# Chunked linear attention and a mixture of experts on one core: domain probabilities over ScalarE's queue, loads in the order of chunks, and a new order of work

## The chip, the cores and the metric

The kernel runs on one core of a Trainium2 chip. TensorE (PE) multiplies matrices into PSUM; VectorE (DVE), ScalarE (ACT) and GpSimd (POOL) do the elementwise work; SyncE (SP) issues nearly all DMAs. Each engine works through its own list of instructions in order, and waits on semaphores for the others. The metric is the device time of one execution in microseconds (us). Three runs of the kernel before took 286.79, 284.99 and 287.0 us: median 286.79. One more execution was recorded by the profiler.

## The reference

Five inputs feed a linear attention with a state (4 batches, 8 heads, 768 positions, head size 48), whose output goes through a mixture of 4 experts (3072 rows of 384, inner size 1024):

```python
for t in range(S):
    kt, vt, rt = k[:, :, t], v[:, :, t], r[:, :, t]
    cur = einsum('bhd,bhe->bhde', u[None] * kt, vt)
    y[:, :, t] = einsum('bhd,bhde->bhe', rt, state + cur)
    state = w[None, :, :, None] * state + einsum('bhd,bhe->bhde', kt, vt)
x = y.transpose(0, 2, 1, 3).reshape(B * S, H * D)
p = domain_probs / (domain_probs.sum(-1, keepdims=True) + 1e-09)
for e in range(E):
    out += p[:, e:e + 1] * (maximum(x @ w1[e], 0.0) @ w2[e])
```

## The kernel before, in words

**Attention.** The sequence is cut into 24 chunks of 128 positions: chunk `ci` is batch `ci % 4`, place `ci // 4`. A chunk needs its r, k and v, 192 KB each (L271). r and k are multiplied by powers of w (`scale`, L433 or L438, on DVE; for chunks 1 to 3 partly on POOL) and turned (`T`): chunks 0 to 7 by PE transposes (L502) and a copy out of PSUM (`Tout`, L80 on ACT or L82 on DVE), later ones by a DMA transpose (L483). `At` is the product of k and r per head (L550), on half the height of the array. `mask` (L564, L567) keeps the upper triangle. `Y` multiplies it by v in bf16 (`Vb`, L80 on ACT or L84 on POOL) and adds the state's part (L590, L597). The u term goes over POOL and DVE: `ruk_a` (L450), `ruk_b` (L458), `dcoef` (L471), `dv` (L476); `Yout` (L612) adds dv to Y. `Sm` (L666), `Sv` and `S` carry the state on.

**Experts.** The first six chunks ("plain": chunks 0 to 3 together, 4 and 5 as halves) are transposed on PE (`X`, L649) and copied (`Xout`); `l1` is x @ w1 (L756, L762, L1180), `relu` its copy on ACT (L771, L773, L1185), `l2` the product with w2 (L792, L1197), and `ev` (L736, L738) multiplies by p and adds. The other chunks are multiplied by p first (`Xs`, L626, into four buffers in two halves that each chunk reuses) and turned by DMA (`Xout`, L637); they form stages 2 to 5 of four chunks and stage 6 of two. There the second product is made of products `P` with sums of weights (`mix`, L860) and sums of activations (`sum`, L933), L969 on PE, in the order of SEQ_2 to SEQ_5. w1 and w2 come in pieces (w1e0.1 is piece 1 of expert 0's w1; L288, L291) into four staging buffers, and are cast to bf16 by ACT, DVE or POOL (`cast`).

**p.** `prow`, 24 rows of 512 numbers (48 KB), is loaded by SP (L302) after the w2 pieces of expert 0. `pt` (L384) turns it by four fp32 transposes on PE, and `pn` (L388 to L391) normalises it on DVE.

**Order.** No order is written out by hand. Everything is a job with the engines that can do it, a rank, needs and buffers, and a planner in the kernel (L1249 to L1404) goes through an imagined time and hands each free engine the ready job of the lowest rank; what it makes is then issued as it stands. So ranks (`NUDGE` adds to some), the list of loads `ORDER`, and `GATES` (which job of the experts a pair of later chunks has to wait for) change the order on all engines. Where the planner sees PE without work in the first 20 us, it fills in spin matmuls (L247) that compute nothing (L1410 to L1418); they are instructions like others, and run whether or not the next job is ready.

```python
            if t < 20 and n > 0:
                spin(n, 1)
```

Of the kernel before, what the change touches and what calls it, by code (L numbers as in the profile page):

```python
# [19 lines left out]
def kernel(  # L20
# [121 lines left out]
    GATES = [0, 9, 1, 3, 15, 23, 26, 26]  # L142
# [16 lines left out]
    for n, sc in enumerate(ORDER_SC):  # L159
        CH0[sc], SC_AT[sc], X_AT[sc] = ci, at, n % 2  # L160
        for x in range(2 if sc == 6 else 4):
# [32 lines left out]
    SEQ_4 = ((0, 1, 0), (1, 1, 0), (0, 2, 0), (0, 2, 1), (0, 1, 1), (0, 7, 0), (0, 6, 0), (0, 6, 1), (0, 7, 1),  # L194
             (0, 5, 0), (0, 5, 1), (1, 2, 0), (1, 1, 1), (0, 3, 0), (0, 3, 1), (0, 4, 0), (0, 4, 1), (1, 2, 1),
             (1, 7, 0), (1, 6, 0), (1, 6, 1), (1, 7, 1), (1, 5, 0), (1, 5, 1), (1, 4, 0), (1, 4, 1), (1, 3, 0),
             (1, 3, 1))
    SEQ_5 = ((0, 1, 0), (1, 1, 0), (0, 7, 0), (0, 1, 1), (2, 2, 2), (1, 1, 1), (0, 6, 0), (0, 6, 1), (1, 7, 0),
             (2, 2, 1), (0, 7, 1), (2, 2, 7), (0, 5, 0), (0, 5, 1), (1, 6, 0), (2, 2, 4), (0, 4, 0), (1, 6, 1),
             (0, 4, 1), (1, 7, 1), (2, 2, 6), (0, 3, 0), (1, 5, 0), (1, 5, 1), (1, 4, 0), (2, 2, 5), (1, 3, 0),  # L200
             (1, 4, 1), (2, 2, 3), (0, 3, 1), (1, 3, 1))
# [11 lines left out]
             ('l1', 3, 1, 0, 1): -20, ('l1', 3, 6, 6, 2): 8, ('sum', 6, 1, 2, 1): -20, ('C', 6, 1, 2): 20}  # L213
# [39 lines left out]
    def load_job(name, nbytes_us, run, takes=(), needs=()):  # L253
        q_rank[0] += 1
        job(name, {"S": 0.5}, run, needs, q_rank[0], takes, (), nbytes_us)
# [3 lines left out]
    def load_in(n, ci):  # L259
# [12 lines left out]
        load_job((n, ci), (0.965, 64), run, (("inp", ci),))  # L272
# [28 lines left out]
    def load_p():  # L301
        load_job("prow", (0.36, 2), lambda: nc.sync.dma_start(  # L302
            prow, moe_domain_probs.rearrange("(n p) e -> n p e", p=C)))

    ORDER = ("K0 K1 R0 R2 R1 V0 K2 w1e0.1 w1e0.0 w1e0.2 V1 K3 V2 R3 w2e0.0 V3 w2e0.1 w2e0.2 p K4 w1e1.1 "
             "w1e1.0 R4 w2e1.0 w1e1.2 R5 V4 w2e1.1 w2e1.2 K5 K6 K7 K8 R9 R13 R6 w1e2.2 V5 K11 w1e3.2 "
             "w1e3.0 V12 V6 R7 w1e3.1 K10 R8 w2e2.1 K9 R16 w1e2.0 w1e2.1 K18 K15 V7 w2e2.0 w2e2.2 R12 V9 "
             "V16 R10 R17 R15 V14 V8 K14 K17 R18 w2e3.0 w2e3.1 w2e3.2 V17 V11 K13 R11 V10 V13 V15 K16 R14 "
             "K12 V18 " +
             " ".join(f"c{i}" for i in range(19, TOTC))).split()  # L310
    for what in ORDER:
        if what == "p":
            load_p()
        elif what[0] == "c":
            for n in ("Rt", "Kt", "Vt"):
                load_in(n, int(what[1:]))
        elif what[0] in "RKV":
            load_in(what[0] + "t", int(what[1:]))
        else:
            for i in ([int(what[5:])] if what[4:] else range(len(PIECES))):  # L320
                load_w(int(what[1]), int(what[3]), i)
# [58 lines left out]

    def c_pt():
# [11 lines left out]
    job("pt", {"T": 0.15}, c_pt, ["prow"], 0, (("mm", "pp"),))  # L393
    job("pn", {"V": 1.1}, c_pn, ["pt", ("Yout", SUB - 1)], 3.0, (), (("mm", "pp"),))
# [646 lines left out]
    def mix2(m, k):  # L1041
# [13 lines left out]
        needs = all_cast + [("Yout", ci) for ci in range(TOTC - SUB, TOTC)] +             ([("mix", 4, hf) for hf in range(2)] if m == 4 else [])  # L1055
# [10 lines left out]
    def level2(sc, at0):  # L1066
# [4 lines left out]
        def one(m):  # L1071
# [5 lines left out]
            def summed2(k, hf):  # L1077
# [10 lines left out]
                needs = all_cast + [("Yout", ci) for ci in range(TOTC - 2, TOTC)] + [("relu", e, sc, fb, 0) for e in (2 * hf, 2 * hf + 1) for fb in range(NFB)] +                     ([("sum2", sc, m, {3: 1, 2: 3, 4: 2}[k], hf)] if k != 1 else [])  # L1088
# [220 lines left out]
    def start(e):  # L1309
# [16 lines left out]
        if got is not None and now < HURRY:  # L1326

            us = got.on[e]
            for i in soon[e]:
                if i.name not in gone and i.rank < got.rank and fits(i) and                         now < known[i.name] < now + 0.6 * us:  # L1330
# [123 lines left out]
```

## Time and profile before

| what | us |
|---|---|
| median of three runs | 286.79 |
| lowest and highest of them | 284.99, 287.0 |
| the profiled execution's own time | 284.42 |
| its span, first to last instruction | 282.6 |
| PE busy (share of the span) | 277.0 (98%) |
| ACT, DVE, POOL busy | 188.4, 182.7, 112.2 |
| granted TensorE clock, mean | 0.999 |
| spin matmuls, all before 19 us | 95 |

Times in the profile are us from the start of the span. Busy time of PE takes in spins, and the ends of matmuls are modelled, so small gaps between them show only as the distance from one start to the next. A row of the waits names who waited, for whom, and total, times and longest. In the timeline and the chain of waits a row begins with start and duration.

### The profile page before, as it was taken

The numbers are of one execution on the slowest core, as the hardware profiler recorded it, in microseconds if no ns is written. First come the engines' busy times: TensorE is split into PE (matmuls) and PEld (weight loads), VectorE is DVE, ScalarE is ACT, GpSimd is POOL, SyncE is SP. The second block draws the span as 40 slices with busy tenths as digits, with TensorE's granted clock in tenths as the row PEclk, the third lists the DMA queues.
The fourth block names the chain that finished last, engine by engine and source line by source line (L and its number), as shares of the span: only waits on it lengthen the run. The fifth ranks groups of instructions, "written<-read, shape, count | busy, mean of one in ns | idle before, by whom it ended". The sixth has DMA issues, their size and how long they took to land.

```text
span 282.6 us, 6933 instructions
## 1 busy us (share of the span) xinstructions
PE 277.0 (98%) x2794; PEld 200.3 (71%) x2794; DVE 182.7 (65%) x313; ACT 188.4 (67%) x351; POOL 112.2 (40%) x129
## 2 busy tenths in 40 slices
PE   8989999999999999999999999999999999999995
PEld 3778567675865445899445899445899544999895
DVE  5976879875687667786347786167785353681061
ACT  4775946898652788655988656879653799612840
POOL 2884456882527565357463346264230000000000
PEclk9999999999999999999999999999999999999999
DMA  7999999999999999493993494965539110401001
GB/s 159 287 247 322 252 273 263 260 264 202 264 201 251 208 199 204 81 165 86 201 209 76 83 171 77 209 127 102 96 70 162 62 28 0 77 25 70 30 14 44
DMA packets 133491, 43.23 MB, mean 153 GB/s; under 512 B 121658, under 2 KB 133436, under 8 KB 133460
## 3 DMA queue, kind: packets, MB, share of 16 engines
q1 hardware_dynamic: 133300, 42.74, 70.0%
q8 instruction: 22, 0.36, 0.5%
q14 instruction: 9, 0.07, 0.1%
q10 hardware_dynamic: 160, 0.05, 0.1%
HBM read 26.79 MB, written 4.72 MB: 112 GB/s over the span
## 4 chain that ended last, share of the span: by engine, by line
PE 88%; DMA 5%; SPq 3%; DVE 1%; ACT 1%; issue 0%; POOL 0%; DVEq 0%; ACTq 0%
PE hT_ps L762 32%; PE M_ps L969 29%; PE out_ps L792 8%; DMA Vt<-in_v_dram 4%; PE hT_ps L1180 4%; PE hT_ps L1214 4%; PE out_ps L1197 3%; SPq L271 2%; PE Y_ps L597 2%; PE At_all L550 2%; PE hT_ps L756 1%; PE Y_ps L590 1%; PE St_ps L666 1%; DMA RKin<-in_r_dram 1%; PE M_two L1127 1%; PE RKT_ps L502 1%
## 5 line engine op out<-in xcount | busy, mean ns | idle before, releaser
L773 ACT ACTIVATE hAll<-hT_ps 128x512 bf16<-128x512 f32 x152 | 88.5, 598 | 13.6 <-PE hT_ps L762 8.6
L762 PE MATMUL hT_ps<-stg,w_sb 128*128 128x512 bf16 x384 | 86.7, 379 | 0.1
L762 PEld LDWEIGHTS <-w_sb 128*128 128x128 bf16 x456 | 42.8, 98 | 48.1 <-issue 0.4
L969 PEld LDWEIGHTS <-hAll 128*128 128x128 bf16 x832 | 68.5, 98 | 1.0
L626 ACT ACTIVATE stg<-dv,p_nat 128x384 bf16<-128x384 f32 x72 | 41.6, 609 | 12.6 <-DMA stg<-stg 6.8
L450 POOL TENSOR_TENSOR ruk<-RKin 128x384 f32<-128x384 f32 x24 | 27.1, 1129 | 41.9 <-DMA RKin<-in_k_dram 21.6
L969 PE MATMUL M_ps<-w_sb,hAll 128*128 128x192 bf16 x400 | 37.6, 246 | 0.0
L1004 ACT COPY o_sb<-M_ps 128x192 f32<-128x192 f32 x35 | 11.1, 317 | 37.4 <-PE M_ps L969 37.3
L476 POOL TENSOR_TENSOR dv<-Vt,dcoef 128x384 f32<-128x384 f32 x24 | 24.6, 1024 | 26.5 <-ACT stg L626 25.3
L458 POOL TENSOR_TENSOR ruk<-ruk,U_sd 128x384 f32<-128x384 f32 x23 | 26.5, 1153 | 1.4
L685 POOL TENSOR_TENSOR S<-Tn,wC 64x192 bf16<-64x192 f32 x32 | 21.4, 669 | 13.7 <-DVE Tn L675 12.2
L933 DVE TENSOR_TENSOR hAll<-hAll 128x1024 bf16<-128x1024 bf16 (+1 forms) x30 | 24.2, 825 | 0.2
L792 PE MATMUL out_ps<-w_sb,hAll 128*128 128x384 bf16 x128 | 23.9, 326 | 0.0
L933 DVE TENSOR_TENSOR stg<-hAll 128x1024 bf16<-128x1024 bf16 (+1 forms) x15 | 12.7, 847 | 15.3 <-ACT hAll L1222 11.5
L438 DVE TENSOR_TENSOR RK_sb<-RKin,W_both 128x768 bf16<-128x768 f32 x16 | 17.1, 1078 | 7.8 <-DMA RKin<-in_r_dram 4.7
L969 PE MATMUL M_ps<-o_sb,hAll 128*128 128x192 bf16 x216 | 21.6, 246 | 0.0
L969 PE MATMUL M_ps<-w_mix,hAll 128*128 128x192 bf16 x216 | 21.1, 246 | 0.0
L933 DVE TENSOR_TENSOR hAll<-stg,hAll 128x1024 bf16<-128x1024 bf16 (+1 forms) x15 | 12.6, 851 | 9.8 <-PE M_ps L969 9.6
L567 DVE TENSOR_TENSOR AtM<-At_all,mask 128x1024 bf16<-128x1024 f32 x8 | 9.8, 1221 | 12.6 <-PE At_all L550 12.6
L762 PE MATMUL hT_ps<-xTe,w_sb 128*128 128x512 bf16 x72 | 17.2, 379 | 0.0
L1006 DVE TENSOR_TENSOR o_sb<-o_sb,M_ps 128x192 f32<-128x192 f32 x25 | 8.8, 350 | 11.7 <-PE M_ps L969 9.4
L792 PEld LDWEIGHTS <-hAll 128*128 128x128 bf16 x128 | 11.6, 98 | 6.3
(110 smaller groups left out, 377.3 us busy)
## 6 DMA issues: line engine op xcount, KB each, us to landing
stg<-in_moe_w_dram SPq DMA_DIRECT2D x16, 576.0 KB, 6.2
RKin<-in_k_dram SPq DMA_DIRECT2D x24, 192.0 KB, 3.5
RKin<-in_r_dram SPq DMA_DIRECT2D x24, 192.0 KB, 3.6
Vt<-in_v_dram SPq DMA_DIRECT2D x24, 192.0 KB, 4.3
out_dram<-o_sb SPq DMA_DIRECT2D x23, 192.0 KB, 2.2
stg<-in_moe_w_dram SPq DMA_DIRECT2D x8, 384.0 KB, 5.7
stg<-stg SPq DMA_TRANSPOSE x36, 2.8
RKT<-RK_sb SPq DMA_TRANSPOSE x16, 3.5
```

The source lines that it names most:

```text
L438: job(("scale", ci, 0), {"V": SCALE_US}, lambda: nc.vector.tensor_mul(RK[:, :, :, 0:D], tl["in", ci], W_both), [("Rt", ci), ("Kt", ci), (" ...
L450: nc.gpsimd.tensor_mul(tl["ruk", ci], tl["Rt", ci], tl["Kt", ci])
L458: nc.gpsimd.tensor_mul(tl["ruk", ci], tl["ruk", ci], U_sd)
L476: nc.gpsimd.tensor_mul(tl["dv", ci], tl["Vt", ci], tl["dcoef", ci].to_broadcast((128, H, D)))
L626: nc.scalar.mul(o, tl["Ysb", ci], p_nat[:, e, n_p:n_p + 1])
L685: nc.gpsimd.tensor_mul(S_new[pr, :, cl], Tn2[pr, tn_at[ci], :, cl], wC[pr, :, None].to_broadcast((P2, NP, D)))
L762: nc.tensor.matmul(ps[:, 0:n, :].rearrange("p a b -> p (a b)"), w1_sb[:, e, db, fb * 128:(fb + 1) * 128], xTe[:, x0 + db, s0:s0 + n, :].re ...
L773: nc.scalar.activation(hTs[:, fb, s0:s0 + n, :], ps[:, 0:n, :], AF.Relu)
L792: nc.tensor.matmul(ps, relu_tile(e, sc)[:, fb, s, :], w2_sb[:, e, fb, :], start=(fb == 0), stop=(fb == NFB - 1))
L933: nc.vector.tensor_tensor(o, x, y, op=op)
L969: nc.tensor.matmul(tl["P", sc, q, m], st, moving(m, hf, (n + 4) % 8), start=(opens and n == 0), stop=(hf == 1 and n == 7), skip_group_chec ...
L1180: nc.tensor.matmul(ps[:, f, :], w1_sb[:, e, db, (a + f) * 128:(a + f + 1) * 128], get_xTe(1)[:, db, s, :], start=(f == 0 and db == 0), sto ...
```

## The change

p is no longer an entry of `ORDER` on SP: ACT issues its load right after the logarithm of w. `pt` waits for `umm` as well, its planned cost goes from 0.15 to 0.85, and it gets a pad of 2.2 us in the planner; `pn` no longer waits for `Yout` of chunk 3. Each load of r, k or v from chunk 5 on now comes behind the same load of the chunk before. `ORDER`, `GATES`, SEQ_2 to SEQ_5 are given anew (SEQ_5 keeps its second level), nine entries are added to `NUDGE`. The other edits only break long lines.

In the planner's order on the engines this does the following. In PE's, pt goes from between chunk 0's l2 pieces to between T(1,0) and Y(0), and the first l1 of expert 0 from between At(1) and At(2) to behind Y(1). On POOL dv(0) goes behind ruk_b(1), two scales, ruk_a(2) and ruk_b(2). On DVE pn goes ahead of chunk 1's masks. There are 93 spins for 95. SP's list is the same up to the last w2 piece of expert 0.

```diff
-    GATES = [0, 9, 1, 3, 15, 23, 26, 26]
+    GATES = [3, 9, 0, 11, 6, 5, 7, 30]
...
-    SEQ_4 = ((0, 1, 0), (1, 1, 0), (0, 2, 0), (0, 2, 1), (0, 1, 1), (0, 7, 0), (0, 6, 0), (0, 6, 1), (0, 7, 1),
...
+    SEQ_4 = ((0, 1, 0), (0, 2, 0), (0, 2, 1), (0, 1, 1), (0, 7, 0), (1, 1, 0), (0, 6, 0), (0, 6, 1), (0, 7, 1),
...
-             ('l1', 3, 1, 0, 1): -20, ('l1', 3, 6, 6, 2): 8, ('sum', 6, 1, 2, 1): -20, ('C', 6, 1, 2): 20}
+             ('l1', 3, 1, 0, 1): -20, ('l1', 3, 6, 6, 2): 8, ('sum', 6, 1, 2, 1): -20, ('C', 6, 1, 2): 20,
+             ('Wsb', 1): -2, 'lnr': 2.1, ('dv', 0): 27.8, ('Xout', 1): 14.5, ('mask', 2, 0): -4,
+             ('T', 3, 0): -11.8, ('Sm', 15): -20, ('mix', 2, 0): 20.1, ('l1', 0, 0, 6, 3): -9.1}
...
-    def load_job(name, nbytes_us, run, takes=(), needs=()):
+    def load_job(name, nbytes_us, run, takes=(), needs=(), behind=()):
         q_rank[0] += 1
-        job(name, {"S": 0.5}, run, needs, q_rank[0], takes, (), nbytes_us)
+        job(name, {"S": 0.5}, run, needs, q_rank[0], takes, (), nbytes_us, behind)
...
-        load_job((n, ci), (0.965, 64), run, (("inp", ci),))
+        load_job((n, ci), (0.965, 64), run, (("inp", ci),), (), ((n, ci - 1),) if ci > SUB else ())
...
-    def load_p():
-        load_job("prow", (0.36, 2), lambda: nc.sync.dma_start(
-            prow, moe_domain_probs.rearrange("(n p) e -> n p e", p=C)))
-
-    ORDER = ("K0 K1 R0 R2 R1 V0 K2 w1e0.1 w1e0.0 w1e0.2 V1 K3 V2 R3 w2e0.0 V3 w2e0.1 w2e0.2 p K4 w1e1.1 "
-             "w1e1.0 R4 w2e1.0 w1e1.2 R5 V4 w2e1.1 w2e1.2 K5 K6 K7 K8 R9 R13 R6 w1e2.2 V5 K11 w1e3.2 "
...
+    ORDER = ("K0 K1 R0 R2 R1 V0 K2 w1e0.1 R5 w1e0.0 K7 w1e0.2 V1 K3 R7 V2 R3 R9 w2e0.0 R18 V3 w2e0.1 "
+             "w2e0.2 K4 w1e1.1 w1e1.0 R10 R8 R4 w2e1.0 K8 w1e1.2 w2e1.1 V4 K5 w2e1.2 w1e2.2 K16 R13 V11 "
...
+    job("prow", {"A": 0.5}, lambda: nc.scalar.dma_start(
+        prow, moe_domain_probs.rearrange("(n p) e -> n p e", p=C)), ["ln"], -98)
...
-    job("pt", {"T": 0.15}, c_pt, ["prow"], 0, (("mm", "pp"),))
-    job("pn", {"V": 1.1}, c_pn, ["pt", ("Yout", SUB - 1)], 3.0, (), (("mm", "pp"),))
+    job("pt", {"T": 0.85}, c_pt, ["prow", "umm"], 0, (("mm", "pp"),))
+    jobs["pt"].pad = 2.2
+    job("pn", {"V": 1.1}, c_pn, ["pt"], 3.0, (), (("mm", "pp"),))
```

## The prediction

> **What bounds the kernel now.** I read the page's busy shares first, then TensorE's waits, then the stretches, and the chain of waits last. The busy shares name the engine:
>
> ```profile
> PE 277.0 (98%) x2794; PEld 200.3 (71%) x2794; DVE 182.7 (65%) x313; ACT 188.4 (67%) x351; POOL 112.2 (40%) x129
> ```
>
> No other engine is above 71%, so a term counts only if it changes what PE does or when PE can begin. All of PE's waits in 282.6 us are these, apart from what hides inside modelled ends:
>
> ```profile
> PE spin_ps L247 <- DVE hAll L89: 1.1, 1, 1.1
> PE Y_ps L597 <- ACT Vb L80: 0.7, 1, 0.7
> PE At_all L550 <- DVE RKT L82: 0.2, 1, 0.2
> ```
>
> All three lie before 17 us. "Busy" hides more, because the spin matmuls of L247 are filler and count as work. In the stretches (columns: length, then busy time and instructions of PE, PEld, DVE, ACT, POOL, then clock, DMA share, GB/s) the start looks almost full:
>
> ```profile
> 0.00:10.00 10.00, 8.61 (x68) 4.84 (x69) 6.72 (x24) 5.43 (x11) 3.94 (x12) 1.00 0.85 182
> 10.00:20.00 10.00, 9.04 (x156) 7.52 (x153) 8.13 (x17) 6.67 (x12) 8.83 (x10) 1.00 1.01 269
> 20.00:30.00 10.00, 10.00 (x132) 7.89 (x130) 7.02 (x18) 6.51 (x14) 5.88 (x7) 1.00 1.09 331
> ```
>
> So I took the starts of PE's matmuls and subtracted, for each, the usual step of its kind (0.056 us for 128 columns, 0.162 for 384, 0.216 for 512), with nothing allowed to spins. What is left is lost time: 6.25 us in the first 10 us, 5.49 us in the next 10, 0.63 us from 20 to 30, and 5.2 us in the remaining 250. Nearly all of the last two figures is one fixed cost, 0.09 us on entering and leaving each block of half-height At matmuls (0.3 to 0.4 us for a pair) or of fp32 transposes. Only one late gap is a wait, 0.27 us at 99.4 us. The chain of waits shows whose:
>
> ```profile
> 94.52 4.25 DMA Vt<-in_v_dram
> ...
> 98.84 0.51 ACT Vb L80
> 99.36 0.51 ACT hAll L773
> ...
> 99.90 0.38 PE hT_ps L762
> ```
>
> Chunk 13's v lands late; its Vb copy stands on ACT between two relus, and PE runs out of PSUM buffers behind it. So there are 11.7 us of start, most of it unavoidable; one stall of 0.27 us; and 261 us of matmul work (the same jobs in both PE orders). The reader should see how little there is to win, and that any new wait is paid in full.
>
> **Part 1: p.** Before, SP issues p at 18.35 us (0.58 us of SP), its 24 packets of 2 KB move from 22.3 to 23.9 us, and PE transposes it in the middle of dense work:
>
> ```profile
> 24.42 0.65 PE L792 MATMUL out_ps<-w_sb,hAll 128*128 128x384 bf16 x3
> 25.00 0.65 PE L384 MATMUL p_ps<-hAll 24*128 24x24 f32 x4
> 25.59 0.50 PE L792 MATMUL out_ps<-w_sb,hAll 128*128 128x384 bf16 x2
> ```
>
> Three 384-column matmuls take 0.49 us, so PE is free at 24.91 and resumes at 25.59: the transposes cost 0.68 us of dense time. Afterwards they stand between T(1,0) and Y(0), near 9.3 us. Y(0) must wait for chunk 0's second mask (DVE, over at 10.19) anyway, so T(1,0) over at 9.29 plus 0.68 is 9.97, and the transposes are hidden. Gross gain: 0.68 us.
>
> They now wait for p over ScalarE's queue, issued after the Ln that ends at 3.90. That queue's w, issued at 1.44, had landed when Ln began at 3.38, thus in 1.94 us; p on SP took 5.5 us from issue to last packet. So p comes between 5.8 and 9.4 us. I take 6.5, nearer to w because it is the same queue. Behind pt on PE stand Y(0), T(1,1), T(2,·), At(1). Even 9.4 plus 0.68 is 10.1, before Y(0) may begin; later than that, each us costs at most one us. On ACT the issue (0.53 us for w) fits into the 1.65 us that ACT then waits for w_ps.
>
> The row for SP's issue, 0.58 us, is all that leaves SP, and SP is waiting for buffers or for room in its queue there. The Trainium skill ("DMA: Bandwidth & Descriptors", section "Issuing engines are not separate DMA queues") says that DMAs from different engines share the same 16 DMA engines, and that a second issuer saves only the issue time. It speaks against a gain from the queue itself: by it, the change of queue alone is worth at most that 0.58 us of SP and 0 on PE.
>
> pn, four small DVE operations, ran from 25.69 to 26.80: 1.11 us. It now stands on DVE after chunk 1's RKT copy. Behind it are chunk 1's masks, which wait for At(1), and PE puts 5 and then 19 spins (24 × 0.056 = 1.34 us) ahead of that. DVE ends pn at about 12.7, At(1) at 13.3: hidden, with 0.6 us of cover.
>
> **Part 2: the first chunks, walked.** On POOL dv(0) goes from third to eighth place: ruk_b(1) 8.61 to 9.61, two scales to 11.6, ruk_a(2) and ruk_b(2) to 13.6, dv(0) to 14.4 (before: 9.44). Yout(0) follows at 15.0 instead of 11.2, X(0) at 15.1 instead of 11.4, and the first expert matmuls (L756 before) at 16.6 instead of 13.6. What covers this is the load of chunk 1's v:
>
> ```profile
> 8.33 7.25 DMA Vt<-in_v_dram
> ...
> 15.61 0.52 ACT Vb L80
> ...
> 16.17 0.37 PE Y_ps L597 x8
> ```
>
> The SP order up to that load is the same. The order afterwards puts 9 + 9 + 6 expert matmuls into the gaps behind Y(1), where the old order had spins. With Y(1) at 16.35 (At(2) waits for mask(1,1), over at 15.65), X(1), T(3,1) and the third group follow; the second group waits for ACT's cast of w1, over at 17.45 plus 0.15. T(3,0) then starts at about 19.05, before 19.21. By then pt is done (0.68 more), and Y(2) is still to come (0.20): PE is 0.64 us ahead in work.
>
> Not all of it survives. The last third of l2 for chunk 0 needs POOL's third w2 cast:
>
> ```profile
> 23.23 1.96 POOL L84 CAST w_sb<-stg 128x1152 bf16<-128x1152 f32 x2 [0.67 <-DMA stg<-in_moe_w_dram]
> ```
>
> That is a DMA wait and then 1.96 us, to 25.19, and the loads ahead of it are unchanged. PE reached that matmul at 25.59; the new order would reach it at 24.95 and must wait until 25.25. **The start gives 0.34 us**, between 0 (a p packet stream that pushes the loads) and 0.68 (cast early).
>
> **Part 3: orders after 25 us.** The work is equal, so only waits matter. The new ACT order has Vb 9, 10 and 12 ahead of the relus of stage 2 and none between the first sixteen: the 0.27 us stall goes (range 0 to 0.27, if the relu before is late next). R5 goes ahead of w1e1.0: one 192 KB load, at the 250 GB/s of that slice 0.8 us later. Its cast began at 30.0 on ACT, so it had landed by then; 0.8 later, and 0.8 for the cast on DVE, where it now stands, makes 31.6, and l1(1,0,0,0), the first to use it, began at 32.6: 1 us of cover, and without it the cost is what is over. w1e2.1 and w1e3.2 are now needed 12 and 16 us earlier in PE's work, but are issued 3.1 MB earlier and 0.3 MB later. w1e3.2's issue began at 40.5; with 5.7 to land, 1.3 for the 0.3 MB and a cast of 0.82 us it is ready by 48.4, and its new use is at about 52: 3.6 us of cover. k, r, v in chunk order: SP's waits for POOL at L271 are 0.5, 0.5 and 0.3 us, on an engine that nobody waits for there; 0. The product orders change sums on DVE (65% busy); 0, with up to 1 us for a sum that comes late.
>
> **Sum.** 284.42 (the profiled run; its span of 282.6 plus 1.8 around it) − 0.34 − 0.27 = 283.8. The median of the runs shown, 286.79, is 2.4 us above the profiled run; taken from it the same 0.6 us gives **286.2**.
>
> **Rivals.** (a) *Slower: the start of stage 2 waits for its last transposes.* Y(9), the last chunk of that stage, now has five l2 blocks, Sm(9) and one plain half behind it before stage 2's first matmul: 5 × 1.30 + 0.17 + 0.67 = 7.3 us of PE, where the last one had nine blocks and 0.34, 12.0. The path is Yout 0.8, two Xs 1.2, Xout(8,1) ahead of it on SP 0.2, and issue to landing 3.3: 5.5, so 1.8 us to spare. If Xs(9,0) waits for its y_e buffer as L626 did once for a DMA (4.31 us), and landing takes 1 us more, PE stands 3.5 us: 284.42 − 0.6 + 3.5 = 287.3, **289.7** on the median's scale. It decides from 1.8 us of lateness. For it: the shortened cover. Against: those buffers are freed six us of PE work earlier.
> (b) *p lands late.* For it: SP's p took 5.5 us. At 8 us, as if queued behind several loads, it comes at 11.9; pt holds PE until 12.6 instead of 10.2, and with 0.8 us absorbed by the load of v the start loses 1.6: **287.8**. Against: w's 1.94 us.
> (c) *Nothing is gained*: another wait eats the 0.68 us, and the stall comes back at another Vb. **286.8**.
> (d) *Faster: v of chunk 1 is no bound.* Where the longer runs lose their 2.4 us I cannot see; if in waits that the later X(0) and the new load order avoid, all of it and the 0.6 go: **283.8**.
>
> **How the numbers follow.** Forecast 0.50 (its own range 285.2 to 287.0), (c) 0.12, (b) 0.08, (a) and its like at other stage starts 0.18, (d) 0.12. A measurement of this kernel tells about 1%, 2.9 us, from no change. All of (d) counts as faster: 0.12. Slower: (a), with 0.02 of the forecast's half for stalls that I don't foresee, 0.20. Within: the rest, 0.68. The range runs from 283.8 to 290.0, a little above (a).
>
> **What would show it.** Right: p_ps near 9.3 us, no gap at p_ps, out_ps steps of 0.162 us across 25 us; a wait of about 0.3 us ahead of the last third of l2 for chunk 0; dv(0) near 13.6; no PE gap between 92 and 103 us. Wrong: PE waiting for L391's DMA; spins ending after their successor was ready; any gap over 0.3 us at the first L770 of a stage.

## The result, and the profile after

The changed kernel takes **287.0 us** (median of 20 runs, 286.01 to 288.2); the kernel before, run beside it, took 285.74 us (median of 20, 284.8 to 287.5). The ratio is 1.0045, with a 95% interval from 1.0029 to 1.0061: slower by 1.3 us. Run again beside the kernel before (e6 below), it was slower by 0.8 us: 287.06 against 286.29, ratio 1.0029 [1.0009, 1.005]. The forecast was 286.2 us, 0.6 us below the median known then; its range of 283.8 to 290.0 holds the time, but its sign is wrong.

The profiled execution took 286.78 us, with a span of 285.0 us. The busy shares of the page:

```profile
PE 277.6 (97%) x2792; PEld 200.4 (70%) x2792; DVE 193.9 (68%) x314; ACT 187.0 (66%) x348; POOL 115.1 (40%) x131
```

VectorE does one instruction more than before and is busy 11.2 us longer (6.8 in a second pair of profiles). A part is work: three casts of 1152 columns more, of 0.75 us at the least, and a smaller cast and a copy less, about 1.2 us together. The rest is the same instructions taking longer, and it is the first sign of what went wrong. TensorE's waits (engine, line, for whom; total, times, longest in us) have two new rows:

```profile
PE St_ps L674 <- DVE y_sb L620: 1.4, 1, 1.4
PE spin_ps L257 <- DVE hAll L89: 1.1, 1, 1.1
PE hT_ps L770 <- DVE w_sb L82: 1.0, 1, 1.0
```

The spins' row was there before. The first and the third are Sm(5), which waits for Yout(5), and l1(1,0,0,0), which waits for cast(1,1,0); both wait for VectorE. The stretches (columns as before: length, busy time and instructions of PE, PEld, DVE, ACT, POOL, then clock, DMA share, GB/s):

```profile
0.00:10.00 10.00, 8.73 (x58) 4.73 (x58) 6.42 (x24) 5.09 (x10) 4.22 (x13) 1.00 0.84 178
10.00:20.00 10.00, 9.68 (x166) 8.41 (x167) 8.98 (x20) 7.45 (x14) 8.51 (x10) 1.00 1.02 276
20.00:30.00 10.00, 10.00 (x132) 7.67 (x130) 6.46 (x15) 6.51 (x14) 5.84 (x7) 1.00 0.94 254
30.00:40.00 10.00, 9.00 (x71) 4.71 (x70) 9.12 (x12) 6.75 (x11) 4.19 (x5) 1.00 0.91 282
40.00:50.00 10.00, 10.00 (x123) 7.34 (x120) 10.00 (x17) 5.01 (x8) 5.83 (x8) 1.00 1.07 242
50.00:60.00 10.00, 8.64 (x103) 5.86 (x101) 10.00 (x15) 8.12 (x13) 9.70 (x10) 1.00 0.93 256
```

The last three rows in the kernel before:

```profile
30.00:40.00 10.00, 10.00 (x81) 5.60 (x79) 7.91 (x12) 7.43 (x13) 4.08 (x5) 1.00 1.02 251
40.00:50.00 10.00, 10.00 (x127) 7.25 (x125) 9.42 (x17) 6.30 (x10) 6.48 (x8) 1.00 1.00 263
50.00:60.00 10.00, 10.00 (x128) 7.64 (x128) 8.95 (x16) 8.71 (x15) 9.05 (x9) 1.00 1.05 279
```

The reader should look at VectorE, the third of the busy times: 9.12, 10.00 and 10.00 us of 10, where the kernel before had 7.91, 9.42 and 8.95. TensorE, 10.00 in all three before, falls to 9.00 and 8.64 in the first and the last of them. The start itself went nearly as reckoned; p_ps, reckoned near 9.3, came 0.4 us later:

```profile
9.69 0.54 PE L391 MATMUL p_ps<-hAll 24*128 24x24 f32 x3
```

p's packets on ScalarE's queue moved from 4.5 to 5.3 us; dv(0) began at 13.79 (reckoned 13.6), X0 at 15.27 (15.1), the first expert matmul at 16.57 (16.6), T(3,0) at 19.05 (19.05), and the first matmul of the second expert at 29.80, 0.57 us ahead of the 30.37 of before (in the second pair of profiles at 31.16 against 31.00). The chain of waits shows where the end is decided. In the kernel before it is TensorE's own work alone from 19.21 us to 88.6 us:

```profile
19.21 0.40 PE RKT_ps L502 x4
...
88.65 0.63 DVE o_sb L738
```

Now it reads:

```profile
17.28 5.72 DMA stg<-in_moe_w_dram
...
23.05 1.94 POOL w_sb L84 x2
...
25.25 2.40 SPq L298
...
28.27 7.49 DMA stg<-in_moe_w_dram
...
35.79 0.96 DVE w_sb L82
...
47.31 2.62 DVE RK_sb L441 x3
...
50.70 0.98 DVE RK_sb L446
...
52.37 0.56 DVE y_sb L620
...
52.97 0.33 PE St_ps L674 x4
```

It goes from a weight load through GpSimd's casts and an issue on SyncE (2.40 us; the same load's issue had taken 2.96 us in the kernel before, but had ended 2.6 us earlier) into another weight load, from there at 35.79 us into VectorE, and it stays on VectorE for 17 us until Sm(5).

Lost time, reckoned as in the prediction (the distance between matmul starts less the usual step), from two profiles of each kernel:

| us lost by TensorE | before | before again | after | after again |
|---|---|---|---|---|
| 0 to 40 us | 12.60 | 12.52 | 12.52 | 13.11 |
| 40 to 90 us | 1.16 | 1.18 | 2.95 | 2.69 |
| 90 us to the end | 3.80 | 4.40 | 3.53 | 3.54 |
| the two fp32 matmuls of u (L354; after, L358), not in the rows above | 0.70 | 1.39 | 1.39 | 1.32 |
| start of the last matmul to the span's end | 3.38 | 3.38 | 3.69 | 3.67 |
| the executions' own times | 284.42 | 285.57 | 286.78 | 287.05 |

The means of the pairs differ by +0.26, +1.65 and −0.57 us in the lost time. So nothing was won at the start, 1.65 us were lost between 40 and 90 us, and the stall at stage 2, which the prediction wanted gone, is gone (0.27 us at 99.4 in the one profile of before, 0.69 us at 100.1 in the other, none in either after).

u's matmuls add +0.31 and the end +0.30, 1.95 in all, where the times differ by 1.92 (these executions stand further apart than the medians, 1.3 and 0.8). u's matmuls are chance: they take 0.70 us in six of the twenty profiles, of both kernels and their edits, and up to 1.39 in the others. The 0.30 us at the end are not: after the last store GpSimd pauses for about 0.3 us between two of the instructions that close the program. The pause is in all fourteen profiles in which GpSimd has 197 or 198 records in the trace, waits included (the changed kernel and twelve of its edits), always ahead of the 197th, and in none of the six with 190 (the kernel before, e4, e10, e18, and e7 and e11, edits of the changed one). What the pause is stays open.

### The profile page after: what moved, and what is told of

Same layout as the page of the kernel before. It is cut to its first block, busy times and chain, and to the rows that moved or that the text cites. A ratio compares the mean times of both kernels' runs of the same rounds, so it can differ in the third digit from the quotient of the medians.

```text
span 285.0 us, 6934 instructions
## 1 busy us (share of the span) xinstructions
PE 277.6 (97%) x2792; PEld 200.4 (70%) x2792; DVE 193.9 (68%) x314; ACT 187.0 (66%) x348; POOL 115.1 (40%) x131
## 4 chain that ended last, share of the span: by engine, by line
PE 82%; DMA 6%; DVE 5%; SPq 2%; POOL 2%; issue 1%; ACT 0%
PE hT_ps L770 33%; PE M_ps L977 28%; DMA stg<-in_moe_w_dram 5%; PE hT_ps L1224 4%; PE out_ps L800 4%; PE hT_ps L1190 3%; PE out_ps L1207 3%; DVE RK_sb L441 1%; PE At_all L558 1%; DMA RKin<-in_r_dram 1%; PE Y_ps L605 1%; PE spin_ps L257 1%; SPq L281 1%; PE Y_ps L598 1%; PE St_ps L674 1%
## 5 line engine op out<-in xcount | busy, mean ns | idle before, releaser
L770 PEld LDWEIGHTS <-w_sb 128*128 128x128 bf16 x456 | 42.3, 98 | 47.6 <-DVE w_sb L82 1.6
L977 PEld LDWEIGHTS <-hAll 128*128 128x128 bf16 x832 | 68.6, 98 | 1.0
L484 POOL TENSOR_TENSOR dv<-Vt,dcoef 128x384 f32<-128x384 f32 x24 | 22.4, 934 | 26.1 <-ACT stg L634 24.2
L693 POOL TENSOR_TENSOR S<-Tn,wC 64x192 bf16<-64x192 f32 x32 | 22.6, 708 | 22.2 <-DVE Tn L683 20.7
L466 POOL TENSOR_TENSOR ruk<-ruk,U_sd 128x384 f32<-128x384 f32 x23 | 27.9, 1215 | 1.3
L941 DVE TENSOR_TENSOR hAll<-hAll 128x1024 bf16<-128x1024 bf16 (+1 forms) x30 | 25.6, 866 | 0.2
L941 DVE TENSOR_TENSOR stg<-hAll 128x1024 bf16<-128x1024 bf16 (+1 forms) x15 | 14.5, 967 | 12.8 <-ACT hAll L1232 11.4
L446 DVE TENSOR_TENSOR RK_sb<-RKin,W_both 128x768 bf16<-128x768 f32 x16 | 19.2, 1221 | 1.8 <-DMA RKin<-in_k_dram 1.8
L770 PE MATMUL hT_ps<-xTe,w_sb 128*128 128x512 bf16 x72 | 18.0, 379 | 1.0 <-DVE w_sb L82 1.0
L479 DVE TENSOR_REDUCE dcoef<-ruk 128x8 f32<-128x384 f32 x24 | 12.9, 543 | 6.0 <-POOL ruk L466 5.8
L620 DVE TENSOR_TENSOR dv<-Y_ps,dv 128x384 f32<-128x384 f32 x18 | 10.0, 554 | 10.3 <-PE Y_ps L605 10.2
```

What stands on the lines that cost most here:

```text
L446: job(("scale", ci, 0), {"V": SCALE_US}, lambda: nc.vector.tensor_mul(RK[:, :, :, 0:D], tl["in", ci], W_both), [("Rt", ci), ("Kt", ci), (" ...
L466: nc.gpsimd.tensor_mul(tl["ruk", ci], tl["ruk", ci], U_sd)
L479: nc.vector.reduce_sum(tl["dcoef", ci], tl["ruk", ci], axis=AX.X)
L484: nc.gpsimd.tensor_mul(tl["dv", ci], tl["Vt", ci], tl["dcoef", ci].to_broadcast((128, H, D)))
L693: nc.gpsimd.tensor_mul(S_new[pr, :, cl], Tn2[pr, tn_at[ci], :, cl], wC[pr, :, None].to_broadcast((P2, NP, D)))
L770: nc.tensor.matmul(ps[:, 0:n, :].rearrange("p a b -> p (a b)"), w1_sb[:, e, db, fb * 128:(fb + 1) * 128], xTe[:, x0 + db, s0:s0 + n, :].re ...
```

## The experiments

The edits below were made on the finished order of the planner: `move(x, y)` issues job x directly behind job y, on another engine if a third argument names one. All other orders stay as they are. Ratios are to the kernel before, run on the same chip in the same hour; its median was 286.44, 286.29, 286.38, 286.29 and 285.64 us in the five groups of runs.

**First theory: two casual orders on VectorE.** Ahead of each late instruction stand others that could go behind it: scale(8,0) ahead of Yout(5), S(3) and scale(5,0) ahead of cast(1,1,0).

```diff
 e1
+    move(("scale", 8, 0), ("Yout", 5))
 e2
+    move(("cast", 1, 1, 0), ("scale", 4, 1))
 e3
+    move(("cast", 1, 1, 0), ("scale", 4, 1))
+    move(("scale", 8, 0), ("Yout", 5))
```

> The changed kernel with one instruction moved on DVE alone: the r and k scale of chunk 8 goes from ahead of Yout(5) to directly behind it. Theory (DVE's order is the cause): Yout(5) starts at about 50.0 us instead of 52.4, Sm(5) on PE no longer waits (1.35 us in the changed kernel's waits), and the kernel gets 1.2 to 1.5 us faster: 285.6 on the scale where the changed kernel has 287.0. Rival (loads are late in any case, one wait only hides another): Yout(5) or the next use of a late load waits as long, and the time stays within 0.4 us of 287.0.

> The changed kernel with one instruction moved on DVE alone: the cast of piece 0 of expert 1's w1 goes ahead of S(3) and of the scale of chunk 5. Theory (the cast stands behind other work on DVE although its load has landed by 29.8 us): the cast starts at about 31.2 instead of 32.4, PE's wait of 1.0 us at 33.85 goes, and l1 for expert 1 starts 0.8 to 1.2 us earlier; but the wait at 51 us hangs on a load that comes when it comes, so it grows by as much, and the time stays within 0.4 us of 287.0 (this move alone gives nothing). Rival (the load of that piece is what is late, pushed by chunk 5's r): the cast has to wait for its DMA and PE's wait at 33.85 stays.

> Both moves together. Theory (the two waits are the whole loss, and what the change gains at the start and at 99 us remains): 287.0 - 1.2 - 1.4 = 284.4, that is 1.0 to 1.5 us under the kernel before (285.74). Rival (late loads): no better than the kernel before, 285.7 or more, with new PE waits between 33 and 60 us.

Measured: e1 286.71 us, ratio 1.0015 [0.9996, 1.0034]; e2 286.99, 1.0029 [1.0011, 1.0048]; e3 286.67, 1.0014 [0.9988, 1.004]. Each wait that was aimed at went from its place, and others took over or stayed: in e1 and e3 T(7,0) waited instead, at 55 to 56 us, for Xout(5), which stands later on VectorE's list, and in e2 the wait at Sm(5) stayed at 1.4 us. The waits of e3:

```profile
PE RKT_ps L510 <- DVE xTe L82: 1.3, 1, 1.3
PE spin_ps L257 <- DVE hAll L89: 1.1, 1, 1.1
PE RKT_ps L510 <- DVE RK_sb L441: 0.5, 1, 0.5
```

Some 0.1 to 0.3% may have been won (the intervals overlap or touch those of the changed kernel), but not the 2.6 us that the theory had for e3. A wait that moves when its cause is moved suggests that the engine as a whole is late, not that one instruction stands badly.

**p alone, in the kernel before.**

```diff
 e4 (before)
+    prow_job.run = lambda: nc.scalar.dma_start(...)
+    pt_job.on = {"T": 0.85}
+    move("prow", "ln", "A")
+    move("pt", ("T", 1, 0))
+    move("pn", ("Tout", 1, 1))
...
```

> The kernel before with p's part of the change alone: p issued by ScalarE behind the logarithm, its four transposes between T(1,0) and Y(0) in the place of 15 spins, pn behind chunk 1's RKT copy; every other instruction where it was. Theory: 0.3 us faster than the kernel before (0.68 of dense PE time saved, part of it lost at l2's wait for the third w2 cast), 285.4. Rival (pn on DVE, 1.1 to 1.7 us in the start, delays the masks and PE): 0.3 us slower or more, 286.0 and up.

Measured: 286.76 us, 1.0027 [1.0002, 1.0052]. The gain does not come: pn now delays chunk 1's copy and masks on VectorE, for which TensorE waits (`At_all` for `RKT`, 1.3 us). The first matmul of the second expert that its trace holds is at 30.82 us (one ahead of it is missing), against 30.37 and 31.00 in the two profiles of the kernel before. p's 0.68 us do not show alone, and with the rest of the new order the next wait takes them.

**GpSimd beside VectorE.** In the changed kernel SyncE issues r of chunks 6, 7 and 8 one behind the other:

```profile
42.37 2.60 SPq L281 DMA_DIRECT2D RKin<-in_r_dram  x3
```

In the kernel before these issues began at 35.05, at 42.83 and, behind that of chunk 9, after 47.46. Now GpSimd runs their ruk products without a pause, while VectorE runs scale(6,0), scale(7,1), scale(7,0) and scale(8,0). All of them read two operands from SBUF. Timelines of the changed kernel (start, duration, instruction), VectorE and then GpSimd:

```profile
47.31 3.46 DVE L441 TENSOR_TENSOR RK_sb<-RKin,W_both 128x384 bf16<-128x384 f32 x3
50.70 1.75 DVE L446 TENSOR_TENSOR RK_sb<-RKin,W_both 128x768 bf16<-128x768 f32 x1
52.37 0.55 DVE L620 TENSOR_TENSOR y_sb<-Y_ps,dv 128x384 bf16<-128x384 f32 x1
```

```profile
46.82 2.26 POOL L458 TENSOR_TENSOR ruk<-RKin 128x384 f32<-128x384 f32 x2
49.05 2.59 POOL L466 TENSOR_TENSOR ruk<-ruk,U_sd 128x384 f32<-128x384 f32 x2
51.60 1.71 POOL L458 TENSOR_TENSOR ruk<-RKin 128x384 f32<-128x384 f32 x1
```

Of the three scales in the first row two take 1.35 us each, where one alone takes 0.55; the wide one takes 1.75, where 0.95 is usual; GpSimd's products take 1.31 and 1.71 for 1.00. The same line of code in the two kernels, by its minimum, median and longest in ns, before and then after:

```profile
L433 DVE TENSOR_TENSOR RK_sb<-RKin,W_both x8: 547/550/1356, 29.0 to 53.6; 128x384 bf16<-128x384 f32 x8
```

```profile
L441 DVE TENSOR_TENSOR RK_sb<-RKin,W_both x8: 545/1145/1352, 28.8 to 49.4; 128x384 bf16<-128x384 f32 x8
```

Same instruction, same shape, eight times each: the median went from 550 to 1145 ns; three of the eight took over 0.9 us before, six after. Yout (0.55 us) and dcoef (0.54 us), which take one operand from SBUF, kept their durations beside the same products; the cast of 1152 columns, which also takes one, is not settled (1.55 us beside a product, but 0.76 and 1.35 with GpSimd idle). The Trainium skill ("SBUF — State Buffer", section "Who interferes with whom") says that a VectorE instruction with two SBUF inputs contends with a GpSimd instruction that reads SBUF; it calls the ports that they share an exclusive lock, and the order of issue decides who blocks. These rows agree with it, the pairs running as if by turns.

The planner in the kernel has a price for this pair (`SHARED`, L178), but applies it only after 85 us of its imagined time (`LATE`, L177 and L1358), so it put the products beside the scales at no price.

Four runs tested whether that is the cause at 51 us. e5 and e8 put GpSimd's products elsewhere, e7 undoes the load list, and e6 is the changed kernel once more.

```diff
 e5
+    move(("ruk_a", 7), ("dv", 6))
+    move(("ruk_b", 7), ("ruk_a", 7))
+    move(("ruk_a", 8), ("ruk_b", 7))
+    move(("ruk_b", 8), ("ruk_a", 8))
 e8: the same, and
+    move(("cast", 1, 1, 0), ("scale", 4, 1))
 e7
-    ORDER = ("K0 K1 R0 R2 R1 V0 K2 w1e0.1 R5 w1e0.0 K7 ...
+    ORDER = ("K0 K1 R0 R2 R1 V0 K2 w1e0.1 w1e0.0 w1e0.2 ...
```

> The changed kernel with only GpSimd's order touched: the two ruk products of chunks 7 and the two of chunk 8 are issued behind dv(6), so that four of the five back-to-back products (0.99, 1.31, 1.31, 1.31, 1.71 us in the changed kernel's trace) no longer run beside VectorE's scale(6,0), scale(7,1), scale(7,0), scale(8,0). Theory (GpSimd and VectorE slow each other, and the adjacent loads of chunks 6 to 8 bunched them): the scales fall from 1.35 and 1.75 to about 0.55 and 0.97 us, Yout(5) is at about 50.5 in place of 52.4, TensorE's 1.5 us wait at Sm(5) goes; 1.2 to 1.5 us below the changed kernel, about 285.6. Rival (it is VectorE's own order, four scales ahead of Yout(5), whatever GpSimd does): the scales stay long and the wait stays, 287.0. The wait at l1(1,1,0,0), 1.2 us at 32.5, stays by both.

> The changed kernel once more, unchanged, beside the others on one chip. Both theories: ratio to the kernel before about 1.0045, with the two waits of 1.2 us (at the second expert's first matmul) and 1.5 us (at Sm(5)) in its trace. If either wait is missing from this trace while the ratio is the same, it belongs to one execution only and explains nothing.

> The changed kernel with the load list of the kernel before (k, r, v of later chunks again spread between the weights), p's path, gates and nudges as in the changed kernel. Theory (bunched loads bunch GpSimd's products on top of VectorE's scales): GpSimd's products of chunks 6, 7, 8 stand apart again, the scales are 0.55 us, Sm(5)'s wait of 1.5 us goes; the cast that l1(1,1,0,0) waits for is still on VectorE behind the scales of chunk 4 in this kernel, so the 1.2 us at 32.5 may stay: about 285.6. Rival (p's path or the gates are the cause, the load order is not): 287.0, waits as in the changed kernel.

> The changed kernel with GpSimd's four products behind dv(6) and the cast(1,1,0) directly behind scale(4,1) on VectorE, S3 and scale(5,0) behind it. Theory (the two waits are the whole of what was lost): both go, 2.0 to 2.7 us below the changed kernel, 284.4 to 285.0, so 0.4 to 0.7 per cent below the kernel before. Rival (VectorE is short of time as a whole in the first 90 us, a wait that goes comes back later): 286.5 or more, with another wait of TensorE on VectorE between 50 and 90.

Measured: e5 289.71 us, 1.0121 [1.0083, 1.0158]; e6 287.06, 1.0029 [1.0009, 1.005]; e7 296.37, 1.0353 [1.0306, 1.0399]; e8 289.66, 1.0131 [1.0089, 1.0172]. In e5 the mechanism was as the theory had it: scale(7,0) took 0.54 us, scale(8,0) 0.95, Yout(5) was at 51.01 and the wait at Sm(5) was gone. The time was not, because of what the edit did besides. dv(6), behind which the products now stand, waits for chunk 6's v until 52.7 us, and Vb(6) stands behind the products. TensorE's longest wait in e5:

```profile
PE Y_ps L605 <- POOL Vb L84: 2.2, 1, 2.2
```

e6 has the wait at Sm(5) again (1.1 us), but only 0.3 us lost at 33; in its place stands one at 25 us, l2 of chunk 0 for GpSimd's cast of the third w2 piece:

```profile
PE out_ps L800 <- POOL w_sb L84: 1.2, 1, 1.2
PE St_ps L674 <- DVE y_sb L620: 1.1, 1, 1.1
```

So the two losses are of different kinds. The one at 51 us is in both profiles of the changed kernel; the one at the start changes its place from one execution to the next (in the profiles of this family 1.0 to 1.5 us at 25 us, or 0.7 to 2.0 at 33). In the changed kernel itself it is a wait for weights at either place; in some of the edits the one at 33 us is for scale(5,0).

e7 settles nothing on what the load list costs as a whole: its planner finds another order everywhere, and TensorE then loses 1.5 us at 94, 3.1 at 121 and 2.0 at 141 us. For the place at 51 us it speaks for the list: with the old one no product runs between 47.6 and 53.5 us, the three scales from 48 to 54 us take 0.93, 0.54 and 1.23 us, and TensorE waits nowhere over 0.3 us between 40 and 90 us. `ORDER`, `GATES` and `NUDGE` seem to fit one another only as a set.

**The load of chunk 5's r.** In e8 (its profile is of an execution of 292.81 us) the cast that TensorE waits for at 33 us stood at the head of VectorE's list, VectorE was idle for 2.07 us, and the cast still began only at 34.00: it waits for its load, w1e1.0. This load stands behind R5 on SyncE. The issues on SyncE of the kernel before (R4, then w1e1.0) and of the changed one (R4 and R5, then w1e1.0):

```profile
20.89 1.11 SPq L271 DMA_DIRECT2D RKin<-in_r_dram  x1
22.09 2.96 SPq L288 DMA_DIRECT2D stg<-in_moe_w_dram  x1
```

```profile
20.79 4.37 SPq L281 DMA_DIRECT2D RKin<-in_r_dram  x2
25.25 2.40 SPq L298 DMA_DIRECT2D stg<-in_moe_w_dram  x1
```

w1e1.0's issue ends at 25.05 us before and at 27.65 us after: 2.6 us later, for a load of 192 KB. R5's own issue takes 3.17 of the 4.37 us, and the buffer that it writes had been free since 12 us. It ends at 25.16 us, near the end of K4's last packets (25.09; in e18 below 24.64 and 24.82), and before, w1e1.0 in the same place ended at 25.05 (25.14). So it seems to be room in the queue that whichever load stands there waits for, and w1e1.0 now waits once more behind R5; the records don't say so. Meanwhile the DMA engines run dry: 44 and 51 GB/s from 27 to 29 us, where before had 381 and 367. One run moved that load alone in the kernel before, and one moved it back in the changed kernel:

```diff
 e18 (before)
+    move(("Rt", 5), ("Rt", 4))
 e13 (after)
+    move(("Rt", 5), ("wst", 1, 1, 2))
+    move(("cast", 1, 1, 0), ("scale", 4, 1))
```

> The kernel before with one load moved: chunk 5's r from behind w1e1.2 to directly behind chunk 4's r, ahead of the second expert's w1e1.0, as the changed kernel has it. Theory (that load's 1024 short rows hold SyncE's queue): w1e1.0's issue is over 2 to 2.6 us later (27 to 27.7 in place of 25.0) and its last packet 2 to 2.5 us later, near 30.8 in place of 28.3 to 29.0; its cast on ScalarE ends near 32.0, where TensorE comes for it at 32.6 to 33: the time stays within 0.5 us, 286.3 to 286.8. Rival (the load costs only its bytes): 0.8 us later, 29.1 to 29.8, and 286.3.

> The changed kernel with the load of chunk 5's r moved on SyncE's queue from ahead of the second expert's first weight piece to behind w1e1.2 (where the kernel before has it), and cast(1,1,0) on VectorE directly behind scale(4,1), since scale(5,0), which stood ahead of it, now waits for that load. Theory (R5 ahead of w1e1.0 holds SyncE's queue, so that w1e1.0 is issued 2.6 us later, 27.65 in place of 25.04): w1e1.0's issue is over near 25.1, its last packet at 28.3 to 29, the cast is over by 32 and TensorE's wait at l1(1,1,0,0) (1.2 to 2.0 us, or in other executions 1.0 to 1.3 at 25 with 0.2 to 0.6 here) goes; the wait at 51 stays: 286.0 to 286.5. Rival (the cast waits for VectorE, not for the load): the wait stays as when the cast alone was moved; 287.0.

Measured: e18 285.9 us, 1.0020 [0.9999, 1.0041]; e13 286.72, 1.0021 [0.9998, 1.0044]. The issues of e18:

```profile
20.48 4.16 SPq L271 DMA_DIRECT2D RKin<-in_r_dram  x2
24.73 2.27 SPq L288 DMA_DIRECT2D stg<-in_moe_w_dram  x1
```

w1e1.0's issue is over at 27.00 us, 2.0 us later than before, its cast on ScalarE then waits 1.32 us for the load, and TensorE loses 0.46 us there; the median is 0.3 us above before, and the ratio's interval holds 1. In e13 the issue is over at 24.79 us, the cast runs from 31.67 to 33.0 without waiting for its load, and TensorE waits neither at 25 nor at 33 us; the wait at Sm(5) stays (1.0 us), and the time is 0.2 us above the theory's range. That R5's place delays w1e1.0's issue is shown in both directions; that it costs time is not clear of noise in either. It is small by itself: in the kernel before, the cast stands on ScalarE, where it has the time.

**Taking the contention away.** e12 shortens GpSimd's products of chunks 7 and 8 to 8 of each head's 48 columns, so that it leaves out most of these chunks' u term; e14 does that and moves R5.

```diff
 e12
+    N_U = 8 if ci in (7, 8) else D
-    nc.gpsimd.tensor_mul(tl["ruk", ci], tl["Rt", ci], tl["Kt", ci])
+    nc.gpsimd.tensor_mul(tl["ruk", ci][:, :, 0:N_U], tl["Rt", ci][:, :, 0:N_U], tl["Kt", ci][:, :, 0:N_U])
...
 e14: the same, and
+    move(("Rt", 5), ("wst", 1, 1, 2))
+    move(("cast", 1, 1, 0), ("scale", 4, 1))
```

> The changed kernel in which the two ruk products of chunks 7 and 8 work on the first 8 of each head's 48 columns only, and dcoef sums those 8 (the bonus term of these two chunks is left incomplete); order and waits are the changed kernel's. GpSimd's four instructions shrink from 1.3 to 1.7 us to about 0.2 us each in their places. Theory (GpSimd's products stretch VectorE's scales): scale(7,0) and scale(8,0) take 0.55 and 0.97 us, Yout(5) is at 51.2 or before, the 1.5 us wait at 51 goes; 285.5 to 286.0. Rival (VectorE is the limit by its order, or a wait that goes comes back behind it): scales as before or a new wait by 60; 286.7 or more.

> The previous edit together with the shortened ruk products of chunks 7 and 8 (8 of 48 columns of each head; the bonus term of these two chunks is incomplete). Theory (the two causes are the queue behind R5 and the products beside VectorE's scales, and they add): neither wait; 285.0 to 285.8, below the kernel before by 0.2 to 0.5 per cent. Rival (the loads set the pace of the first 90 us, so a wait that goes comes back behind it): a new wait of over 1 us by 90, 286.4 or more.

Measured: e12 286.4 us, 0.9998 [0.9967, 1.0029], between its theory and its rival; e14 285.51, 0.9977 [0.9952, 1.0001]. On VectorE in e14, ahead of Yout(5):

```profile
47.62 2.80 DVE L442 TENSOR_TENSOR RK_sb<-RKin,W_both 128x384 bf16<-128x384 f32 x3
50.34 1.07 DVE L447 TENSOR_TENSOR RK_sb<-RKin,W_both 128x768 bf16<-128x768 f32 x1
51.34 0.55 DVE L621 TENSOR_TENSOR y_sb<-Y_ps,dv 128x384 bf16<-128x384 f32 x1
```

The row of three took 2.80 us where it took 3.46, the wide scale 1.07 where it took 1.75, and the wait at Sm(5) is gone in both runs. From the first of these scales to Yout(5) it is 3.72 us, against 5.06 in e13, which has the same instructions in the same order there. Between 40 and 90 us e14 loses 1.50 us, against 2.95 and 2.69 in the changed kernel and 1.16 and 1.18 in the kernel before. e14 stands 1.2 us under e13, its twin with whole products, on the same chip. A part of that is not contention: the two shorter dcoef save 0.68 us of VectorE. They stand behind Yout(5), at 55.25 and 56.58, so the wait at Sm(5) went without them. GpSimd gains time too, but in the changed kernel TensorE waits for nothing of GpSimd between 40 and 60 us. Both parts are time of VectorE, and that is the point: given about 2 us of it, the changed kernel is level with the kernel before or a little below, although e14 has a new wait of 1.4 us at 33.5, T(5,0) for scale(5,0), which now waits for R5. (e12's one profile, an execution of 288.21 us against its median of 286.4, also has a wait of 1.5 us at 72 us, for ScalarE's copy of a later chunk; e14 has 0.3 us there.)

**Can an order do the same?** e9 puts five instructions where the kernel before had them; e15, e16 and e17 move R5 and put off what is not urgent on VectorE.

```diff
 e9
+    move(("cast", 1, 1, 0), ("cast", 1, 1, 1), "A")
+    move(("scale", 8, 0), ("mask", 6, 1))
+    move(("mix", 4, 0), ("scale", 8, 0))
+    move(("ruk_a", 8), ("Vb", 6))
+    move(("ruk_b", 8), ("ruk_a", 8))
 e15
+    move(("Rt", 5), ("wst", 1, 1, 2))
+    move(("cast", 1, 1, 0), ("scale", 4, 1))
+    move(("scale", 8, 0), ("Yout", 5))
+    move(("ruk_a", 8), ("Vb", 6))
+    move(("ruk_b", 8), ("ruk_a", 8))
+    move(("mix", 4, 0), ("Sv", 6))
+    move(("mix", 2, 0), ("mask", 7, 1))
+    move(("dcoef", 8), ("scale", 9, 0))
 e16: as e15, but
+    move(("mix", 2, 0), ("cast", 2, 2, 0))
+    move(("mix", 4, 0), ("Yout", 7))
 e17: as e16, but
+    move(("mix", 4, 0), ("mix", 2, 0))
```

> The changed kernel with five instructions put where the kernel before had them: cast(1,1,0) on ScalarE behind cast(1,1,1); scale(8,0) and then mix(4,0) on VectorE behind mask(6,1) instead of ahead of Yout(5) and Xout(5); ruk_a(8), ruk_b(8) on GpSimd behind Vb(6). Theory (the loss is VectorE crowded at two places, and GpSimd's products on top of it): no wait of TensorE at 32.5 and 51, none over 0.6 us between 30 and 70; 285.0 to 285.8, at or below the kernel before. Rival (VectorE and GpSimd are short of time all through 30 to 70 us, a wait that goes comes back): 286.5 or more, with a new wait at T(7,0) or at Sm(6).

> The edit on R5 and the cast, and at the second place an order that leaves nothing out: scale(8,0) behind Yout(5), mix(2,0) behind mask(7,1), mix(4,0) behind Sv(6), dcoef(8) behind scale(9,0) on VectorE; ruk_a(8) and ruk_b(8) behind Vb(6) on GpSimd. Theory: Yout(5) at 50.7 to 51.4 without the scale of 1.75 us ahead of it, Xout(5) without the mixes of 0.94 and 1.55 us ahead of it, so no wait over 0.5 us between 30 and 70; 285.0 to 286.0, at or below the kernel before. Rival (VectorE short of time to 70 us): a wait of over 1 us on VectorE between 55 and 75; 286.5 or more.

> As the run with R5, the cast, scale(8,0), ruk(8) and the mixes moved, but mix(2,0) stands behind cast(2,2,0) and mix(4,0) behind Yout(7), so that neither is ahead of cast(1,3,0), for which TensorE waited 1.3 us there. Theory (two VectorE queues, around 33 and around 51 to 65 us, and nothing else, made the change slower): no wait over 0.6 us between 20 and 75; 285.0 to 285.9, ratio to the kernel before 0.995 to 0.999. Rival (VectorE is short of time to 75 us, every instruction put off is late elsewhere): a wait of over 1 us between 65 and 80; 286.5 or more.

> The same with both mixes behind cast(2,2,0), ahead of Yout(7), where VectorE had about 1.2 us without work. They take 1.9 us, so Yout(7) comes about 0.7 us later. Theory: 285.0 to 286.2, at most 0.7 us above the run with mix(4,0) behind Yout(7). Rival: Yout(7) is on TensorE's path at once; 0.7 us and more above it, 286.5.

Measured: e9 287.41 us, 1.0033 [1.0011, 1.0054]; e15 286.92, 1.0026 [1.0002, 1.005]; e16 286.78, 1.0033 [1.0014, 1.0052]; e17 286.53, 1.0037 [1.0013, 1.0062]. (In e9 the DMA transpose of chunk 8 stands ahead of the moved scale(8,0), so it turns what its buffer held earlier; chunk 8's attention is not computed from its own r and k.) The wait at Sm(5) is gone in all four and the time is where it was. In e9 the next Sm, at 61.6 us, waits for Yout(6), behind the scale, the mix, another scale and a cast; in e15 TensorE waits at 64 us for cast(1,3,0), behind the two mixes:

```profile
PE hT_ps L770 <- DVE w_sb L82: 1.3, 1, 1.3
```

In e16 and e17 no wait over 0.9 us is left between 40 and 90 us, but several small ones, and at the start the wait for weights is back (1.46 us at 25 us in e16; in e17 1.17 at 33, T(5,0) for the scale that now waits for R5). In e9 and e15 the rival of the expectations was right: what is put off on VectorE comes due before 75 us. In e16 and e17 the time is near the rival's, but its sign is not there: the longest waits behind 65 us are 0.7 and 0.9 us, at 72, and for ScalarE's relu. Where these two lose the rest is not shown. No order that computes everything was found to be clearly faster than either kernel.

**p undone, and the kernel before again.**

```diff
 e11
...
-    job("prow", {"A": 0.5}, lambda: nc.scalar.dma_start(...), ["ln"], -98)
-    job("pt", {"T": 0.85}, c_pt, ["prow", "umm"], 0, (("mm", "pp"),))
-    jobs["pt"].pad = 2.2
-    job("pn", {"V": 1.1}, c_pn, ["pt"], 3.0, (), (("mm", "pp"),))
+    job("pt", {"T": 0.15}, c_pt, ["prow"], 0, (("mm", "pp"),))
+    job("pn", {"V": 1.1}, c_pn, ["pt", ("Yout", SUB - 1)], 3.0, (), (("mm", "pp"),))
```

> The changed kernel with p's part undone (p on SyncE's queue behind w2e0.2, its 0.15 us job without the pad, pn behind Yout(3)); loads in the order of chunks, gates and nudges stay. Theory (the load order bunches the work on VectorE and GpSimd): the four ruk products of chunks 6 to 8 are again side by side with scale(7,0) and scale(8,0) ahead of Yout(5), so the wait at 51 is there; 286.6 to 287.5. Rival (p's place is the cause): no such wait, 286.2 or less.

> The kernel before, unchanged, with a second profile. Both theories: ratio 1.000. Its first profile was an execution of 284.42 us, 2 us below its median. If this profile is near the median, the windows say where its ordinary execution loses the 2 us that the shown one did not: in the start below 35 us, or at the stall ahead of stage 2 (99 us).

Measured: e11 295.6 us, 1.0315 [1.0279, 1.0351]; e10 286.56, 0.9991 [0.9964, 1.0018]. In e11 the wait at Sm(5) is there, with 2.1 us, so it does not need p's new path; and with the new load list the last three scales ahead of Yout(5) take 1.35, 1.34 and 1.75 us there as well. The 9 us are another matter, about half of them this wait, at the first matmul of stage 2:

```profile
PE hT_ps L770 <- DMA stg<-stg: 4.7, 1, 4.7
```

That is the prediction's rival (a), in a kernel where the planner's orders don't fit: a real mechanism, priced at 3.5 us there and measured at 4.7 here, which the changed kernel itself escapes. e10's second profile gives the second column of the table above.

## Why the prediction was wrong, by its own steps

**What bounds the kernel** was right for the kernel before and was taken over for the changed one. "No other engine is above 71%, so a term counts only if it changes what PE does" is a mean over 282 us. From 40 to 60 us VectorE was at 9.42 and 8.95 of 10 already, in the same view that the prediction had used only up to 30 us.

**Part 1 (p) and the walk of Part 2** held to within 0.2 us at dv(0), X0, l1 and T(3,0), and to 0.4 us at p_ps. The rule cited there, that a second issuing engine gives no DMA bandwidth of its own, was not put to a test by any run.

**"Not all of it survives … the start gives 0.34 us"** was the right mechanism with the wrong size. The wait for GpSimd's third w2 cast was put at 0.3 us from one profile; in six profiles of this family it is 1.0 to 1.5 us, and where it is absent the same time is mostly lost at 33 us. Over the two profiles of each kernel the first 40 us lose 0.26 us, where +0.34 was to be won.

**Part 3 failed in two places.** "R5 goes ahead of w1e1.0: … 0.8 us later": it is 2.0 to 2.6 us later, since R5's issue also holds SyncE's queue. The prediction had counted its bytes, and had noted elsewhere that SyncE waits for room in its queue; the kernel's planner even has a model of that room (`RING`, L1272). The "1 us of cover" was thus gone, and the cast's 0.8 us on VectorE was 1.35 (with GpSimd idle beside it; why is open). And "**k, r, v in chunk order: … 0**" is where most of the loss is: 1.65 us between 40 and 90 us. The step looked only for waits on SyncE. It did not ask what the loads set off when they land next to one another: GpSimd's products in one block, on top of VectorE's scales, which then take 1.35 and 1.75 us in place of 0.55 and 0.95. "The product orders change sums on DVE (65% busy); 0" looked at the right engine in the wrong stage. The end of the program stood nowhere in the sum; it took 0.3 us.

**The stall at 99.4 us** went, as reckoned; measured over two profiles it was worth 0.57 us, not 0.27.

**The rivals.** (a) and (b) did not occur. (c), another wait eats p's 0.68 us, describes the start well, but for its second half. The case that did occur, a VectorE that becomes the bound between 30 and 75 us, stood among "stalls that I don't foresee" with 0.02. That the range holds the time, and that 287.0 is only 0.8 us from the forecast, is luck: the base, a median of three, was 1.05 us above the median of twenty (285.74). From that one the forecast would be 285.1, and the miss is 1.9 us.

What stays open: what exactly holds the issue of R5 on SyncE, why the wait for weights falls at 25 us in one execution and at 33 us in the next, and what GpSimd's pause at the end is. How much of the loss a load list with another spacing of chunks 6 to 8, and with gates and nudges fitted to it, would give back was not tried.

## What to carry to other kernels

A change in the order of loads is priced by what the loads set off when they land, not only by the queue that they stand in: walk each engine through the new order with the durations that its instructions have beside the other engines' work. Read the busy shares by stretches of 10 us over the whole part that is re-ordered; an engine at 9.4 of 10 is as good as full, and an instruction put off on it can come due soon after. When a wait moves as soon as its cause is moved, stop moving instructions and look for time on the engine that all of the waits name.

## What the runs showed of the hardware

- Two engines stretch each other: a VectorE product of two SBUF operands takes 0.55 us alone and up to 1.35 us beside GpSimd's products of the same kind (0.95 and 1.75 for twice the size); GpSimd's take 1.00 us alone, and 1.31 or 1.71 there. VectorE's busy time in the profile counts the stretch as work: 193.9 us against 182.7, of which some 1.2 us are instructions that moved to it.
- One more load of 192 KB (1024 rows of 192 bytes) ahead of another on SyncE's queue delayed that one's issue by 2.0 and 2.6 us, where its bytes at the rate of that slice (250 GB/s) are 0.8 us, and the DMA engines fell to 44 and 51 GB/s for 2 us meanwhile (49 and 130 in e18).
- One profile of this kernel is not its ordinary execution: those of the kernel before were of 284.42 and 285.57 us, with a median of all its runs beside the changed kernel of 285.74. Of the difference 0.69 us are two fp32 matmuls at 5.4 us, which took 0.70 us in one and 1.39 in the other, and 0.42 us the stall at stage 2.
- With seven or eight records more on GpSimd's list the end of the program was 0.3 us longer in fourteen of fourteen profiles; no wait that the records name explains it.
